# Transposes of x and of the selected rows in 64-row halves, a whole group of heads per visit

## The chip, the core and the metric

The kernel runs on one core of one Trainium2 chip. The metric is the device time of one execution in microseconds; the median of several runs is compared. TensorE is called PE in the views (PEld is its weight load), VectorE DVE, ScalarE ACT, GpSimd POOL, and SyncE, which issues most of the DMAs, SP. All data is float32.

## What is computed

Eight batches of 12 heads of normalised attention over 448 tokens with heads of 64 columns, and then, for each batch, a mixture of depths: a gate scores the 448 tokens, the 128 best go through a two-layer network of 1024 hidden columns, and the rest pass unchanged.

```
q_n, k_n = q / sqrt(mean(q*q) + 1e-6) * g_q,  k / sqrt(mean(k*k) + 1e-6) * g_k
attn = softmax(q_n @ k_n.T / sqrt(64))           # 8 x 12 x 448 x 448
x = (attn @ v)  as  (8, 448, 12 * 64 = 768)
scores = x @ w_gate                              # 8 x 448
top = indices of the 128 largest scores of a batch
out = x;  out[top] = x[top] + sigmoid(scores[top]) * (relu(x[top] @ w1) @ w2)
```

## The kernel before

The work is 24 groups of heads (8 batches of 3 groups, 4 heads each), and the main loop `for q in range(n_groups)` has a section for each group. In a section PE runs 7 steps; a step is `scores` (L445: keys times queries, 64x64 tiles, 448 columns) for a slice of 64 keys of each head, an exponential on ScalarE (L462), and `values` (L470) into two accumulators. Two steps of scores alternate with two of values, 16 matmul records each. When the last slice is done, `values_out` (L497) copies the two accumulators to SBUF as xT, heads by tokens.

`sum_keys` (L510) sums the exponentials over the keys on PE ("den") into the only bank of `ps_aux`; VectorE has added most of them beforehand (`add_probs`, L493). `invert_sums` (L540) transposes den on PE (L543) and takes the reciprocal on VectorE (L545). `to_tokens(n, c, pool)` (L568) then turns xT of one pair of heads c into x, tokens by columns: four transposes of 128 rows and 112 columns into one bank (L575), and one multiplication with the reciprocals from PSUM to SBUF on VectorE (L577), 112x512. It is called for c = 0 and c = 1 at different places. `after_tokens` schedules the stores of x and the gate products.

Sections 0 to 7 (`q < FIRST`) have two stops, place 0 after four steps and place 1 at the end. At place 0 stand `sum_keys(q - 1)` and pair 1 of group q - 2, at place 1 `invert_sums(q - 1)` and pair 0 of group q - 1, both in the bank of `ps_moe`. From section 8 on all this comes after the 7 steps, at P0, P1 and P2, and each of the three is followed by a piece of the mixture (`step(q, place)`) unless it is in SKIP. A mixture works on two batches at once: `xeT` (L772 to L787) transposes the two gathered blocks of 128 rows, four banks of three transposes of 128x128 each (L777) and four copies on ScalarE (L782); then 7 products for the first layer (L800, 128x128 tiles, `main` in `ps_moe`, `side` in `ps_sc`) and 7 for the second (L870). The fourth mixture and the end of the third run behind section 23.

Between the batches `gate` (L603), `score_rows` (four transposes, L633), `count` (L649), `annotate` and `select` rank the tokens; `select` scatters the chosen rows by POOL's DMA queue and `load_selected` (L699) reads them back on SP.

PSUM has 8 banks: `ps_sc` 4 (scores, side products, x, xeT, score rows), `ps_av` 2, `ps_aux` 1, `ps_moe` 1. A bank is reused when its last reader is done, and the banks of a pool go round in turn.

The order of the work is written out by hand: `at(slot, fn)` puts a piece into a table by due time, in units of sections, and `run(upto)` issues what is due (tables LOADS, PREPARED, STORES, GATES, RANKS). Each engine executes its instructions in the order of issue; DMA issues queue on SP in the same way, so that an issue that waits holds up those behind it. `Loads.load` (L131) keeps 6 buffers for `tok`, the tiles whose squares give the norms; a load into a buffer waits for the square (L345) of its last tile. The norms of the queries go by POOL (L380) and by DRAM (L391, L403) back as a broadcast, and `scale_q` (L409, L412) multiplies the queries with them on VectorE, which the first scores of the group need.

## Time and profile before

| | |
|---|---|
| median of 3 runs | 489.68 us (489.34 to 491.05) |
| the profiled execution | 488.96 us |
| its span | 487.2 us |
| mean granted clock of TensorE | 0.997 of full speed |
| DMA | 118.44 MB, mean 243 GB/s |

The span is the time from the first to the last instruction in the profile; the time of the execution has 1.8 us more. A row of the timeline is a run of equal instructions of one engine: start, length from the first one's start to the last one's end, engine, line, operation, output and inputs, and how many. Matmul records overlap: one lasts 0.27 us or more from issue to the end, while the next begins after its columns have gone through. Sections are found in the timeline by the den matmuls (L520), which stand once in each: place 0 of section 2 is at 42 us, section 8 ends at 131 us, section 23 at 409 us.

### The profile page before, as it was taken

Reading aid. Unit: us, or ns where it says so; the run is one execution under the profiler, and the core shown is the slowest. Engines: PE = TensorE matmul, PEld = TensorE weight load, DVE = VectorE, ACT = ScalarE, POOL = GpSimd, SP = SyncE. Lnnn points to the kernel's source line nnn. Section 1 sums busy time; section 2 is a strip of 40 time slices with the busy share of each in tenths; the row PEclk is TensorE's granted clock in tenths of the full one; section 3 lists DMA queues with packets and bytes.
Section 4 is the critical chain, followed back from the end, with each engine's and each line's share of the span. In section 5 each row is a group of like instructions: output and inputs, shape, how many; then the busy total and the mean of one; then the engine's idle time right before and its main releaser. Section 6 shows DMA issues by size and latency. Waiting matters only on the chain.

```text
span 487.2 us, 11747 instructions
## 1 busy us (share of the span) xinstructions
PE 477.4 (98%) x4708; PEld 294.4 (60%) x4708; DVE 370.2 (76%) x637; ACT 284.8 (58%) x523; POOL 193.2 (40%) x110
## 2 busy tenths in 40 slices
PE   8999999999999999999999999999999999999995
PEld 6554445445578856545557678555456746858962
DVE  5677789867989898998987887889777896753241
ACT  5887887887786566643854865656546574201200
POOL 0785444824652447313846234304183023032002
PEclk9999999999999999999999999999999999999998
DMA  8977879689789976987587876776648404766631
GB/s 300 364 228 279 299 267 277 238 298 320 259 292 369 342 259 193 350 268 266 198 281 283 296 232 230 254 259 219 206 142 279 149 2 122 253 206 249 194 132 71
DMA packets 45121, 118.44 MB, mean 243 GB/s; under 512 B 10275, under 2 KB 10788, under 8 KB 45058
## 3 DMA queue, kind: packets, MB, share of 16 engines
q1 hardware_dynamic: 41442, 110.66, 66.8%
q0 software_dynamic: 3328, 6.71, 4.2%
q8 instruction: 39, 0.64, 0.5%
q10 hardware_dynamic: 288, 0.23, 0.2%
q14 instruction: 24, 0.20, 0.1%
HBM read 93.81 MB, written 31.64 MB: 258 GB/s over the span
## 4 chain that ended last, share of the span: by engine, by line
PE 93%; DMA 4%; DVE 1%; ACT 0%; issue 0%; SPq 0%; POOL 0%; POOLq 0%; DVEq 0%
PE sc L453 26%; PE av L477 25%; PE moe_ps L800 9%; PE moe_ps L870 9%; PE side_ps L870 6%; PE side_ps L800 6%; PE x_ps L575 4%; PE den_ps L520 4%; DMA tok<-in_tok_dram 2%; DMA qT<-in_qT_dram 2%; PE xeT_ps L777 1%; PE row_ps L633 1%; PE den_ps L543 1%; DVE prod L603 0%; ACT sq L345 0%
## 5 line engine op out<-in xcount | busy, mean ns | idle before, releaser
L462 ACT ACTIVATE p<-sc,rinv 128x448 f32<-128x448 f32 x336 | 187.8, 643 | 83.3 <-PE sc L453 63.3
L380 POOL TENSOR_TENSOR rinv<-ss,neg_half 128x14 f32<-128x14 f32 x46 | 131.4, 2869 | 155.1 <-DVE ss L379 145.9
L453 PE MATMUL sc<-qT,kT 64*64 64x448 f32 x1344 | 155.0, 542 | 2.0 <-ACT sq L345 0.8
L477 PE MATMUL av<-p,v 64*64 64x448 f32 x1344 | 151.1, 537 | 0.0
L493 DVE TENSOR_TENSOR sum<-sum,p 128x896 f32<-128x896 f32 x104 | 113.4, 1090 | 5.1 <-ACT p L462 0.8
L477 PEld LDWEIGHTS av<-p,v 64*64 64x64 f32 x1344 | 64.0, 133 | 62.3 <-issue 52.8
L453 PEld LDWEIGHTS sc<-qT,kT 64*64 64x64 f32 x1344 | 58.4, 132 | 65.3 <-issue 42.2
L676 POOL DMA_INDIRECT selected<-x,rank x32 | 41.9, 1308 | 73.2 <-DVE x L668 65.7
L379 DVE TENSOR_REDUCE ss<-sq 128x14 f32<-128x910 f32 x46 | 49.0, 1093 | 8.5 <-ACT sq L345 8.5
L345 ACT ACTIVATE sq<-tok 128x896 f32<-128x896 f32 (+1 forms) x49 | 44.8, 939 | 6.9 <-DVE ss L379 3.4
L577 DVE TENSOR_TENSOR x<-x_ps,rden 112x512 f32<-112x512 f32 x48 | 32.7, 689 | 17.0 <-PE x_ps L575 15.3
L603 DVE SCALAR_TENSOR_TENSOR prod<-x,wg 112x448 f32<-112x448 f32 (+1 forms) x56 | 31.3, 558 | 1.5
L575 PE MATMUL x_ps<-ident,xT 128*112 128x128 f32 x192 | 28.7, 275 | 0.8 <-DVE rden L545 0.8
L412 DVE SCALAR_TENSOR_TENSOR qT<-qT,gg,bc 128x896 f32<-128x896 f32 x22 | 25.2, 1145 | 4.1 <-DMA bc<-rows 2.5
L493 DVE TENSOR_TENSOR sum<-p 128x896 f32<-128x896 f32 x24 | 26.0, 1084 | 2.2 <-ACT p L462 2.2
L500 ACT COPY xT<-av 128x448 f32<-128x448 f32 x48 | 23.2, 535 | 4.4 <-PE av L477 3.0
L575 PEld LDWEIGHTS x_ps<-ident,xT 128*112 128x112 f32 x192 | 21.5, 133 | 5.2 <-issue 2.5
L649 DVE SCALAR_TENSOR_TENSOR cmp<-score_rows,gate,earlier 112x448 f32<-112x448 f32 x32 | 21.8, 683 | 2.3 <-ACT score_rows L639 1.6
L800 PE MATMUL moe_ps<-xeT,ring 128*128 128x128 f32 x192 | 23.1, 277 | 0.0
L800 PE MATMUL side_ps<-xeT,w 128*128 128x128 f32 x192 | 22.8, 275 | 0.0
L743 DVE SCALAR_TENSOR_TENSOR xe<-moe_ps,xe 128x384 f32<-128x384 f32 x14 | 8.6, 616 | 18.2 <-PE moe_ps L870 18.2
L800 PEld LDWEIGHTS moe_ps<-xeT,ring 128*128 128x128 f32 x192 | 22.1, 192 | 0.5 <-issue 0.5
(105 smaller groups left out, 444.5 us busy)
## 6 DMA issues: line engine op xcount, KB each, us to landing
tok<-in_tok_dram SPq DMA_DIRECT2D x47, 448.0 KB
ring<-mixed SPq DMA_DIRECT2D x48, 384.0 KB
kT<-in_kT_dram SPq DMA_DIRECT2D x24, 448.0 KB
v<-in_vp_dram SPq DMA_DIRECT2D x24, 448.0 KB
out_dram<-x SPq DMA_DIRECT2D x16, 672.0 KB
qT<-in_qT_dram SPq DMA_DIRECT2D x23, 448.0 KB
bc<-rows SPq DMA_DIRECT2D x44, 224.0 KB
mixed<-ring SPq DMA_DIRECT2D x16, 384.0 KB
```

The lines of the kernel that those rows point to most:

```text
L345: nc.scalar.activation(out=sq[:, h, :, 0:D], in_=t[:, h], func=AF.Square, scale=scale)
L379: nc.vector.tensor_reduce(out=ss, in_=sq, axis=AX.X, op=OP.add)
L380: nc.gpsimd.tensor_tensor(out=rinv.rearrange(flat), in0=ss.rearrange(flat), in1=neg_half.to_broadcast([128, 2 * NI]), op=OP.pow,)
L453: nc.tensor.matmul(out=scs[hh][D * c : D * (c + 1), 0:S], lhsT=get("kT", n)[r, c, D * i : D * (i + 1)], rhs=get("qT", n)[r, c, :], start=True,
L462: nc.scalar.activation(out=p[:, hh], in_=scs[hh][:, 0:S], func=AF.Exp, scale=rinvs[n, 1][:, hh, i : i + 1],)
L477: nc.tensor.matmul(out=avs[n][c][D * hh : D * (hh + 1), 0:S], lhsT=get("v", n)[r, hh, i, :], rhs=probs[u][r, hh], start=(i == 0), stop=(i ...
L493: nc.vector.tensor_tensor(out=sums[n], in0=probs.pop(u - 1) if begins else sums[n], in1=probs.pop(u), op=OP.add)
L575: nc.tensor.transpose(out=ps[:CP, j, :], in_=t[:, j, :], identity=ident)
L577: nc.vector.tensor_tensor(out=xs[b][:, :, col : col + 128].rearrange("p j (h d) -> p j h d", d=D), in0=ps[:CP].rearrange("p j (h d) -> p j ...
L676: w = nc.gpsimd.indirect_dma_start(out=t[:, :], out_offset=bass.IndirectOffsetOnAxis(ap=rank[:, j : j + 1], axis=0), in_=x[:, j, :], in_of ...
L800: nc.tensor.matmul(out=ps[:, 128 * f : 128 * f + n], lhsT=w[:, d, 128 * f : 128 * (f + 1)], rhs=h[:, d, :n], start=first and f == d == 0, ...
L870: nc.tensor.matmul(out=ps[:n, 0:HD], lhsT=h[:, f, :n], rhs=w[:, f, :], start=first and f == 0, stop=(f == HF - 1), skip_group_check=True,)
```

## The change

- A new helper `transpose_halves` makes two transposes of 64 rows out of one of 128: rows 0 to 63 into one bank, 64 to 127 into another, each against a 64x64 identity. A transpose of x then moves 64 columns, one head, and not 128.
- `to_tokens(n, pools)` handles both pairs of a group at once: 8 double transposes into two banks, then two multiplications on VectorE of the same size as before, one for each bank.
- xeT is transposed in the same way: for each block two banks and six double transposes, two copies each.
- In sections 2 to 7 x is made once, at place 0, for group q - 2: `invert_sums(q - 2)`, `to_tokens(q - 2)`, then `sum_keys(q - 1)`. Place 1 keeps only the score rows, now for all batches.
- From section 10 on x is made at P1 in two banks of `ps_sc`; P2 and `ps_aux` have none any more. Sections 8 and 22 (NEXT) leave theirs to P0 of the section after, before its `sum_keys`.
- `tok` has 5 buffers instead of 6, xT 4 instead of 3. A load of tok is scheduled no earlier than the square of the tile five before. At the start the load of tok (2, 1) goes behind that of v 1.

```diff
-OTHER_BANK = (8, 14, 20, 21)
+NEXT = (8, 22)
-GATES = {8: (10.4, 10.4),
+GATES = {7: (9.75, 9.9),
+ 8: (10.4, 10.4),
-        bufs = {"tok": 6, "qT": 4, "kT": 3, "v": 3}[name]
+        bufs = {"tok": 5, "qT": 4, "kT": 3, "v": 3}[name]
+    def transpose_halves(halves, in_):
+        rows = in_.shape[0]
+        for h, out in enumerate(halves):
+            r = slice(D * h, min(D * (h + 1), rows))
+            nc.tensor.transpose(out=out, in_=in_[r], identity=ident[r, r])
-    load("tok", 2, 1)
     load("v", 1)
-            t = norm_pool.tile([128, NJ, CP], F32, name="xT", bufs=3)
+            t = norm_pool.tile([128, NJ, CP], F32, name="xT", bufs=4)
-    def to_tokens(n, c, pool):
+    def to_tokens(n, pools):
...
-        t = xTs.pop((n, c))
-        ps = bank(pool, [128, NJ, 128], "x_ps")
-        for j in range(NJ):
-            nc.tensor.transpose(out=ps[:CP, j, :], in_=t[:, j, :], identity=ident)
-        col = (n % NG * 2 + c) * 128
-        nc.vector.tensor_tensor(
-            out=xs[b][:, :, col : col + 128].rearrange("p j (h d) -> p j h d", d=D),
-            in0=ps[:CP].rearrange("p j (h d) -> p j h d", d=D),
-            in1=rdens[n][:, :, :, c, None].to_broadcast([CP, NJ, 2, D]),
-            op=OP.mult,
+        halves = [bank(pool, [128, NJ, 2, D], "x_ps") for pool in pools]
+        for c in range(2):
+            t = xTs.pop((n, c))
+            for j in range(NJ):
+                transpose_halves([ps[:CP, j, c, :] for ps in halves], t[:, j, :])
+        x = xs[b][:, :, n % NG * 256 : n % NG * 256 + 256].rearrange(
+            "p j (c h d) -> p j c h d", c=2, d=D
         )
+        for hh, ps in enumerate(halves):
+            nc.vector.tensor_tensor(
+                out=x[:, :, :, hh],
+                in0=ps[:CP],
+                in1=rdens[n][:, :, hh, :, None].to_broadcast([CP, NJ, 2, D]),
+                op=OP.mult,
+            )
+        after_tokens(n)
...
         for i, x in enumerate(xe):
-            for a in range(2):
-                ps = bank(ps_moe if a == i == 0 else ps_sc, name="xeT_ps")
-                for d in range(HC):
-                    dc = HC * a + d
-                    nc.tensor.transpose(
-                        out=ps[:, 128 * d : 128 * d + n],
-                        in_=x[:n, 128 * dc : 128 * (dc + 1)],
-                        identity=ident[:n, :n],
-                    )
+            halves = [
+                (slice(D * h, min(D * (h + 1), n)), bank(pool, [128, 512], "xeT_ps"))
+                for h, pool in zip(range((n + D - 1) // D), (ps_sc if i else ps_moe, ps_sc))
+            ]
+            for dc in range(NDC):
+                transpose_halves(
+                    [ps[:, D * dc : D * dc + t.stop - t.start] for t, ps in halves],
+                    x[:n, 128 * dc : 128 * (dc + 1)],
+                )
+            for t, ps in halves:
                 nc.scalar.copy(
-                    out=xeT[:, i, HC * a : HC * (a + 1), :n],
+                    out=xeT[:, i, :, t],
...
+                t = LOADS.get(("tok", n), n - 5 + P2 if n > 5 else (n - 3) * 0.6)
+                at(max(t, squared_at.get(2 * n + i - 5, 0) + 1e-4), load, "tok", n, i)
...
     keys = squares(0, 1)
+    load("tok", 2, 1)
...
                 if place == 0:
+                    if q > 1:
+                        invert_sums(q - 2)
+                        to_tokens(q - 2, (ps_sc, ps_moe))
                     if q > 0:
                         sum_keys(q - 1)
-                    if q > 1:
-                        to_tokens(q - 2, 1, ps_moe)
-                    if q > NG and g == 1 and b - 1 in GATE_PE:
-                        ranks_of(b - 1)
                 elif q == 0:
                     scale_q_early(1)
-                elif q > 0:
-                    invert_sums(q - 1)
-                    to_tokens(q - 1, 0, ps_moe)
-                    if q > NG and g == 1 and b - 1 not in GATE_PE:
-                        ranks_of(b - 1)
+                elif q > NG and g == 1:
+                    ranks_of(b - 1)
...
         slot[0] = q + P0
+        if q == FIRST:
+            invert_sums(q - 2)
+            to_tokens(q - 2, (ps_sc, ps_moe))
+        if q - 1 in NEXT:
+            if q - 1 == FIRST:
+                invert_sums(q - 2)
+            to_tokens(q - 2, (ps_sc, ps_sc))
         sum_keys(q - 1)
-        if q == FIRST:
-            to_tokens(q - 2, 1, ps_sc)
...
         slot[0] = q + P1
-        invert_sums(q - 1)
-        to_tokens(q - 1, 0, ps_sc)
+        if q != FIRST:
+            invert_sums(q - 1)
+        if q not in NEXT:
+            to_tokens(q - 1, (ps_sc, ps_sc))
         run(q + P1)
         step(q, 1)
         slot[0] = q + P2
-        to_tokens(q - 1, 1, ps_sc if q in OTHER_BANK else ps_aux)
...
     invert_sums(n)
-    to_tokens(n, 0, ps_sc)
-    to_tokens(n, 1, ps_aux)
+    to_tokens(n, (ps_sc, ps_sc))
```

## Rows read from the trace of the kernel before

**Rows 1.** The page, part 1: busy us, share of the span, instructions.

```profile
PE 477.4 (98%) x4708; PEld 294.4 (60%) x4708; DVE 370.2 (76%) x637; ACT 284.8 (58%) x523; POOL 193.2 (40%) x110
```

**Rows 2.** The page, part 4: the chain that ended last, by line.

```profile
PE sc L453 26%; PE av L477 25%; PE moe_ps L800 9%; PE moe_ps L870 9%; PE side_ps L870 6%; PE side_ps L800 6%; PE x_ps L575 4%; PE den_ps L520 4%; DMA tok<-in_tok_dram 2%; DMA qT<-in_qT_dram 2%; PE xeT_ps L777 1%; PE row_ps L633 1%; PE den_ps L543 1%; DVE prod L603 0%; ACT sq L345 0%
```

**Rows 3.** Timeline of PE, section 1: start us, us, engine, line, operation, tiles, count.

```profile
34.50 0.93 PE L477 MATMUL av<-p,v 64*64 64x448 f32 x8
35.36 0.32 PE L543 MATMUL den_ps<-ident,den 128*112 128x128 f32 x1
35.52 0.60 PE L575 MATMUL x_ps<-ident,xT 128*112 128x128 f32 x4
36.05 1.73 PE L453 MATMUL sc<-qT,kT 64*64 64x448 f32 x16
37.60 1.68 PE L477 MATMUL av<-p,v 64*64 64x448 f32 x16
```

**Rows 4.** Timeline of PE, end of section 11 and the scores of 12.

```profile
183.33 0.59 PE L520 MATMUL den_ps<-sum,pick_pair 128*32 128x112 f32 x16
183.85 2.94 PE L800 MATMUL moe_ps<-xeT,ring 128*128 128x128 f32 x24
...
186.74 0.60 PE L575 MATMUL x_ps<-ident,xT 128*112 128x128 f32 x4
187.75 0.65 PE L575 MATMUL x_ps<-ident,xT 128*112 128x128 f32 x4 [0.40 <-DVE rden L545]
188.23 2.84 PE L800 MATMUL moe_ps<-xeT,ring 128*128 128x128 f32 x24
191.00 1.73 PE L453 MATMUL sc<-qT,kT 64*64 64x448 f32 x16
```

**Rows 5.** Groups of instructions by form: busy us, mean ns, idle before.

```profile
L477 PEld LDWEIGHTS av<-p,v 64*64 64x64 f32 x1344 | 64.0, 133 | 62.3 <-issue 52.8 <-ACT xT L500 0.6
...
L575 PE MATMUL x_ps<-ident,xT 128*112 128x128 f32 x192 | 28.7, 275 | 0.8 <-DVE rden L545 0.8
...
L800 PEld LDWEIGHTS side_ps<-xeT,w 128*128 128x128 f32 x192 | 22.1, 192 | 0.0
...
L575 PEld LDWEIGHTS x_ps<-ident,xT 128*112 128x112 f32 x192 | 21.5, 133 | 5.2 <-issue 2.5 <-DVE rden L545 2.2 <-DVE parts L666 0.2
...
L777 PEld LDWEIGHTS xeT_ps<-ident,xe 128*128 128x128 f32 x42 | 4.6, 141 | 0.8 <-issue 0.7
...
L423 PE MATMUL sc<-ident,rinv 64*64 64x64 f32 x112 | 3.6, 221 | 0.0
```

**Rows 6.** Timeline of PE at the start: the products of line 423.

```profile
7.04 1.67 PE L423 MATMUL sc<-ident,rinv 64*64 64x64 f32 x56
```

**Rows 7.** Timeline of DVE: single rows of sections 5, 9 and 11.

```profile
85.17 0.69 DVE L577 TENSOR_TENSOR x<-x_ps,rden 112x512 f32<-112x512 f32 x1 [0.59 <-PE x_ps L575]
...
149.78 1.14 DVE L412 SCALAR_TENSOR_TENSOR qT<-qT,gg,bc 128x896 f32<-128x896 f32 x1
...
187.79 0.69 DVE L577 TENSOR_TENSOR x<-x_ps,rden 112x512 f32<-112x512 f32 x1
...
189.41 1.14 DVE L412 SCALAR_TENSOR_TENSOR qT<-qT,gg,bc 128x896 f32<-128x896 f32 x1
```

**Rows 8.** Timeline of PE: den of section 5, scores of 10, score rows at the end.

```profile
82.43 0.59 PE L520 MATMUL den_ps<-sum,pick_pair 128*32 128x112 f32 x16
...
151.72 1.90 PE L453 MATMUL sc<-qT,kT 64*64 64x448 f32 x16
...
422.16 0.59 PE L633 MATMUL row_ps<-ident,gate 112*112 112x112 f32 x4 [0.43 <-DVE gate L616]
```

**Rows 9.** Timeline of ACT: two squares of tok, the copies of the last xeT.

```profile
147.82 0.95 ACT L345 ACTIVATE sq<-tok 128x896 f32<-128x896 f32 x1 [1.68 <-issue]
...
189.53 0.95 ACT L345 ACTIVATE sq<-tok 128x896 f32<-128x896 f32 x1 [3.37 <-DVE ss L379]
...
443.87 1.63 ACT L782 COPY xeT<-xeT_ps 128x384 f32<-128x384 f32 x4 [17.79 <-PE xeT_ps L777]
```

More of the change, by code (lines that the diff above doesn't have):

```diff
@@ L571, in to_tokens @@
             xs[b] = x_pool.tile([CP, NJ, DX], F32, name="x")
-        t = xTs.pop((n, c))
-        ps = bank(pool, [128, NJ, 128], "x_ps")
-        for j in range(NJ):
-            nc.tensor.transpose(out=ps[:CP, j, :], in_=t[:, j, :], identity=ident)
-        col = (n % NG * 2 + c) * 128
-        nc.vector.tensor_tensor(
-            out=xs[b][:, :, col : col + 128].rearrange("p j (h d) -> p j h d", d=D),
-            in0=ps[:CP].rearrange("p j (h d) -> p j h d", d=D),
-            in1=rdens[n][:, :, :, c, None].to_broadcast([CP, NJ, 2, D]),
-            op=OP.mult,
-        )
-        if c == 1:
-            after_tokens(n)
+        halves = [bank(pool, [128, NJ, 2, D], "x_ps") for pool in pools]
[5 more added lines that the diff above has]
+            "p j (c h d) -> p j c h d", c=2, d=D
+        )
+        for hh, ps in enumerate(halves):
[6 more added lines that the diff above has]
+        after_tokens(n)
     gates, parts, rowss, highers, ranks, slots_dram = {}, {}, {}, {}, {}, {}
@@ L772, in mixture @@
         for i, x in enumerate(xe):
-            for a in range(2):
-                ps = bank(ps_moe if a == i == 0 else ps_sc, name="xeT_ps")
-                for d in range(HC):
-                    dc = HC * a + d
-                    nc.tensor.transpose(
-                        out=ps[:, 128 * d : 128 * d + n],
-                        in_=x[:n, 128 * dc : 128 * (dc + 1)],
-                        identity=ident[:n, :n],
-                    )
+            halves = [
[8 more added lines that the diff above has]
+            for t, ps in halves:
                 nc.scalar.copy(
-                    out=xeT[:, i, HC * a : HC * (a + 1), :n],
-                    in_=ps[:, : HC * 128].rearrange("p (i t) -> p i t", t=128)[:, :, :n],
+                    out=xeT[:, i, :, t],
+                    in_=ps[:, : NDC * D].rearrange("p (i t) -> p i t", t=D)[
+                        :, :, : t.stop - t.start
+                    ],
                 )
@@ L926, in fast @@
     MID, P0, P1, P2 = 0.4, 0.6, 0.75, 0.9
+    squared_at = {}
     def prepare(n):
@@ L946, in prepare @@
         for i in range(2):
+            squared_at[2 * n + i] = times[f"sq{i}"]
             at(times[f"sq{i}"], lambda i=i: sq.setdefault(i, squares(n, i)))
@@ L955, in fast @@
             for i in range(2):
-                at(LOADS.get(("tok", n), n - 5 + P2 if n > 5 else (n - 3) * 0.6), load, "tok", n, i)
+                t = LOADS.get(("tok", n), n - 5 + P2 if n > 5 else (n - 3) * 0.6)
+                at(max(t, squared_at.get(2 * n + i - 5, 0) + 1e-4), load, "tok", n, i)
         if n > 1:
```

## The prediction

> **What bounds the kernel now.** I read the busy times first [rows 1]: TensorE is busy 98% of the span, VectorE 76%, ScalarE 58%. The chain of work that ended last [rows 2] says that TensorE is the bound and not only full: nearly all of the chain is PE lines, and the transposes of x (L575) are 4% of it, some 20 us, those of xeT (L777) 1%. So a microsecond less of PE work is a microsecond less of time, until something that PE now covers comes last; VectorE is the nearest. The PE timeline then shows what a transpose costs and what an interruption costs [rows 3, 4].
>
> **A transpose now.** Four of x take 0.60 us and one alone 0.27, so one follows another in 0.11 us [rows 3, 5]; there are 192, 8 to a group of heads. xeT has 48, 12 to each of four mixtures.
>
> **The halves.** No transpose of 64 rows is in the trace. The nearest rows are the 64x64 products of line 423: two row halves in turn, each into its own bank, 64 columns moving, as in the new helper. 56 of them take 1.67 us and one lasts 0.22, so (1.67 - 0.22)/55 = 0.026 us each, 0.053 a pair [rows 5, 6]; I take 0.055. Eight pairs then take 0.44 us in place of 8 x 0.11 = 0.87: 0.43 saved for each of 24 groups, 10.3 us. xeT: 12 pairs 0.66 in place of 1.31, 0.65 x 4 = 2.6 us. Bounds: 0.053, and 0.11 if the halves run one after another. What differs from line 423 is the stationary side, 112 or 128 columns instead of 64. Its loads last 133 ns (112) and 141 (128) for transposes, 133 (64) and 192 (128) for plain products [rows 5]: 8 ns for 16 columns, 0.5 a column, against 59 for 64, 0.9 a column. 112 columns at 0.5 are 56 ns, about a pair. So I stay near the lower bound.
>
> **The price of another tile shape.** Whenever PE goes from one tile shape to another, the trace has a hole [rows 3]. In section 1, 8 values matmuls from 34.50 should end at 35.25 (16 take 1.50); the den transpose is at 35.36, its record 0.05 longer than 0.27. Four x transposes from 35.52 should end at 35.96; the scores come at 36.05 and their record is 1.73, not 1.68 as the next burst's. Each such change costs about 0.14. Into a plain 128x128 product it is 0.20: moe begins 0.1 late after den (16 take 0.4) and its record is 2.94, not 2.84 [rows 4]. Into den, whose stationary side is 32 columns, I take 0.11. Between x and moe, both of 128 rows, there is no hole now: 188.23 is 0.48 behind an x burst that started 0.05 late [rows 4]. In the new kernel every burst of 64 rows stands between work of other shapes. The trace has no change between 64 and 128 rows at these columns; its price lies between 0 and 0.20, and I take 0.14 in and 0.20 out to a product, since every change of shape that the trace shows costs that. The Trainium skill (TensorEngine Tiling, Key Properties) says that changing the tiling mode, and not just the tile, drains TensorE. The trace agrees for the pairs of shapes it holds; by that rule the price taken stands.
>
> **Section by section** (a section works on one group of heads; its first part ends at place 0, its second at place 1). Section 1: the interruption at place 1 goes, 0.14 + 0.11 + 0.44 + 0.14 = 0.83; the rows give 0.85. Sections 2 to 7: old, x at both places, 0.11 + 0.14 + 0.44 + 0.14 and 0.83, together 1.66 beside the den matmuls; new, one visit: 0.14 + 0.11 (den transpose) + 0.14 + 0.44 + 0.11 + 0.14 = 1.08. Gain 0.58 each; in 4 and 7 the score rows now need an interruption of their own, 0.28, which leaves 0.30. Sum 0.85 + 4 x 0.58 + 2 x 0.30 = 3.8. Section 8: 12 transposes become 8 pairs and group 7 waits for section 9: +0.7. Section 9 takes groups 7 and 8, xeT and six more changes of shape: 2.7 us of such work becomes 2.9, -0.2. Sections 10 to 21: 0.43 - 0.14 - 0.20 = 0.09 each, 0.9 for ten; in 15 and 21, which have xeT, 0.09 + 0.65 - 0.14 = 0.6 each. Section 22 hands its x (0.87) to 23: +0.9; 23 then has two bursts of halves, -0.3. Behind the last section x is shorter by 0.4. All that: 3.8 + 0.7 - 0.2 + 0.9 + 1.2 + 0.9 - 0.3 + 0.4 = 7.4.
>
> **What comes late instead**, each bounded by nothing and by twice the number given.
> - Section 9: scaling group 10's queries on VectorE (L412) ends at 150.92; the scores that need it start at 151.72 [rows 7, 8]. Two more evacuations and a reciprocal for group 7 and two of its gate products (some 3 us) now stand before it there. -1.0.
> - Section 11: a wait of PE goes. The second x burst starts at 187.75, 0.6 late, for the one bank of ps_aux, which rden's reciprocal holds [rows 4]; the new code takes two of ps_sc. But both evacuations (0.69 each) then stand before scaling group 12, now 189.41 to 190.55 with scores at 191.00 [rows 4, 7]: it ends near 191.1. The 0.6 and the 0.09 are lost: -0.2 against the sum.
> - Halves want two banks of ps_sc; where xeT came just before (sections 9, 15, 21), one is held by its second copy, two of four that take 1.63 [rows 9]: -0.35 each, 1.1.
> - Section 5: the den matmuls now wait for a reciprocal issued just before them, since ps_aux has one bank. VectorE was free only 0.59 us before 85.17, while den started at 82.43 [rows 7, 8]; the work moved out of section 4 gives back 1.6. -0.5. At place 0 of the other early sections its queue is shorter.
> - Last section: the score rows at 422.16 already wait for the gate on VectorE [rows 8], whose evacuations end no earlier: the 0.4 is lost.
> - Last xeT: the products behind it needed one copy, now two: both halves ready 0.7 after the start, two copies some 0.85 [rows 9], 1.6 against 1.31 now: -0.3. (Its 0.65 is not in the sum.)
>
> Together 1.0 + 0.2 + 1.1 + 0.5 + 0.4 + 0.3 = 3.5. So 7.4 - 3.5 = 3.9 us.
>
> **Free edits.** VectorE's evacuations stay two of 512 columns to a group, ScalarE's xeT copies four of 384. The fourth xT buffer costs memory only. Five tok buffers instead of six: a load waits on SP until ScalarE has squared the tile five earlier, and SP's later rows, broadcasts and loads queue behind it. The worst, counting loads and squares in the code's order, is tok (14, 1) in section 9: its predecessor is squared at 147.82, its own square is at 189.53 [rows 9], so 40 us of work hide it. At the start tok (2, 1) goes one place back, behind v 1. Price 0, at most 1 us if the first sections then wait for it. The ranks of batch 1 move to place 1 of section 7; the gather that they release on POOL's queue is for the xeT of section 9. Price 0, and if that cover were gone, the 3 us by which they move.
>
> **The sum** against the profiled execution (488.96; span 487.2 and 1.8 around it) is 488.96 - 3.9 = 485.1. That execution lies 0.7 below the median of 489.68, so the forecast is 489.68 - 3.9 = **485.8**, and on its own 483.3 to 488.3: most of the waits absent, or twice as large but for a third.
>
> **Rivals.**
> - *The change of shape to 64 rows is free* where the columns stay 128. Then 22 changes in (0.14), 14 out to products (0.20) and those about xeT (0.8) go: 6.7 us, less some 0.5 that VectorE's scaling then holds up: 479.6. For it: x to moe is free at equal rows. Against: all other changes cost.
> - *VectorE takes most of it.* Scaling ends 0.8 and 0.45 us before the scores in sections 9 and 11; PE that comes earlier waits for it, and in section 5 the reciprocal waits for a whole backlog: another 2.5 us, 488.3. Against: VectorE idles a quarter of the span.
> - *The weight loads bound the pair; slower.* At 0.9 ns a column, as plain loads have it, 112 columns are 0.10 us and 128 are 0.12, so a pair takes what one whole transpose took: the 12.9 us of shorter bursts are gone, the changes of shape stay, and the waits (some 2.5 us) mostly do not arise: 485.8 + 12.9 - 2.5 = 496. It decides from a pair of about 0.08 us on. For it: nothing shows loads of 112 columns side by side. Against: the transposes' loads grow half as fast [rows 5]. The same time comes out if the change does not do what it says and the halves run one after another; line 423 speaks against that [rows 6]. The Trainium skill (TensorE: Matmul & The Clock Gate, LDWEIGHTS) gives columns over 1.2 GHz for a load, whatever its rows; by that estimate 112 columns are 93 ns and this rival holds. The trace has 8 ns for the last 16 columns of a transpose's load where that rule has 13.
>
> **How the numbers follow.** Forecast 0.57, free changes 0.12, VectorE 0.19, weight loads or halves in turn 0.12. Half a per cent, about what a measurement of this kernel can tell from no change, is 2.4 us: faster means under 487.2, slower over 492.1. Faster: four fifths of the forecast, free changes, a little of VectorE's case, 0.60; same 0.27; slower 0.13. The range reaches from 480.0, just above the free changes, to 491.5, past VectorE's case; the slower rival and most of the free changes lie outside, two in ten.
>
> **What will show it.** Eight pairs of x in about 0.44 + 0.2 us as a record: right; near 0.9: the slower rival. The hole between the den transpose and the first half, and between the last half and moe: 0.14 and 0.20, or none. A wait of scores for L412 in sections 9 and 11, of den for L545 in 5. PE starved by tok in the first sections would make the free edits wrong.

## The result, and the profile after

The changed kernel takes 496.17 us (median of 4 runs, 495.82 to 496.98) against 489.51 (488.82 to 491.05) on the same chip: a ratio of 1.0137, 95% interval 1.0121 to 1.0153. It is slower by 1.4%, where 485.8 was forecast, and lies outside the range. The profiled execution took 496.08, its span is 494.4 at a granted clock of 0.998. The page's busy times, and its chain by line:

```profile
PE 477.1 (97%) x4948; PEld 294.3 (60%) x4948; DVE 370.5 (75%) x637; ACT 283.6 (57%) x523; POOL 188.3 (38%) x110
...
PE av L484 11%; PE sc L460 11%; PE moe_ps L883 8%; PE moe_ps L813 7%; PE side_ps L813 4%; PE side_ps L883 4%; PE den_ps L527 1%; PE x_ps L232 1%; DVE x L588 1%; DVE prod L613 1%; ACT xeT L793 1%; PE row_ps L643 0%; DVE xeT L763 0%; PE xeT_ps L232 0%; DVE xe L753 0%
```

Against [rows 1], PE is busy as long as before in a span that is 7.2 us longer: it is not the work that grew. Against [rows 2], this chain holds lines of VectorE and ScalarE between those of PE (L588, L613, L793, L753), and it stops half way through the span, so it can't be read to the start. The waits of PE in the trace of after (us in total, times, longest) say for whom:

```profile
PE sc L460 <- DVE xe L753: 1.9, 3, 1.0
PE row_ps L643 <- DVE gate L626: 1.2, 1, 1.2
...
PE den_ps L527 <- issue: 1.0, 3, 0.4
...
PE sc L460 <- PE moe_ps L813: 0.7, 1, 0.7
```

The first and the third have no like in the kernel before. They don't add up to 7 us, because each idle time is followed by bursts that run longer than before. So I measured sections whole, from the first scores of one to the first scores of the next. "23 and behind" ends with the start of PE's last instruction. The table gives before's length, and then the changes against it in us: as the prediction has them, and as the profiled executions of after and of five of the experiments have them.

| section | before | predicted | after | E1 | E5 | E6 | E8 | last version |
|---|---|---|---|---|---|---|---|---|
| start and 0 | 23.46 | 0 | +0.28 | +0.31 | +0.85 | +0.48 | +2.22 | +0.19 |
| 1 to 3 | 38.63 | -2.01 | -1.73 | -1.74 | -1.73 | -1.79 | -1.75 | -1.80 |
| 4 | 14.17 | -0.30 | +0.06 | +0.06 | +0.06 | +0.39 | +0.06 | -0.03 |
| 5 | 14.17 | -0.08 | **+2.19** | +2.28 | -0.41 | -0.41 | -0.40 | -0.25 |
| 6, 7 | 27.71 | -0.88 | -0.58 | -0.60 | -0.59 | -0.59 | -0.60 | -0.54 |
| 8 | 13.56 | -0.70 | -0.08 | +3.47 | +1.20 | +1.48 | -0.09 | -0.16 |
| 9 | 20.03 | +1.55 | +1.36 | +0.64 | -0.08 | -0.38 | +1.35 | +0.64 |
| 10 | 20.92 | -0.09 | **+0.81** | +1.77 | -0.08 | +0.01 | +0.81 | -0.08 |
| 11 | 18.36 | +0.11 | +0.24 | +0.25 | +0.24 | 0 | +0.25 | +0.24 |
| 12, 16, 17, 18, 20 | 94.40 | -0.45 | -0.48 | -0.46 | -0.48 | -0.10 | -0.47 | -0.46 |
| 13 | 18.65 | -0.09 | **+1.83** | -0.08 | +1.83 | 0 | +1.83 | -0.08 |
| 14 | 18.57 | -0.09 | **+1.86** | -0.34 | +0.18 | -0.49 | +0.19 | -0.34 |
| 15, 21 | 38.02 | -0.50 | -0.26 | -0.25 | -0.25 | 0 | -0.26 | -0.26 |
| 19 | 20.47 | -0.09 | **+1.54** | +0.47 | +1.53 | 0 | +1.54 | +0.46 |
| 22 | 13.14 | -0.90 | -1.00 | -1.00 | -1.00 | 0 | -1.00 | -1.03 |
| 23 and behind | 86.90 | +0.60 | +1.28 | +1.42 | +1.15 | 0 | +1.15 | +0.74 |
| sum | 481.15 | -3.9 | +7.3 | +6.2 | +2.4 | -1.4 | +4.8 | -2.7 |

Five sections are off by nearly a microsecond or more: 5, 10, 13, 14, 19. The others came out within 0.4 us, but for 8 and 23 (0.6 and 0.7).

**The halves themselves.** By form (busy us, mean ns of one, idle before), then PE's timeline of sections 11 and 12, to lay beside [rows 4] and [rows 5]:

```profile
L232 PE MATMUL x_ps<-ident,xT 64*112 64x64 f32 x384 | 16.6, 223 | 0.4
L232 PEld LDWEIGHTS x_ps<-ident,xT 64*112 64x112 f32 x384 | 12.9, 130 | 6.2 <-PE moe_ps L883 1.6 <-issue 1.4 <-ACT xeT L793 0.8
```

```profile
189.13 0.66 PE L232 MATMUL x_ps<-ident,xT 64*112 64x64 f32 x16
189.86 2.94 PE L813 MATMUL moe_ps<-xeT,ring 128*128 128x128 f32 x24
193.54 1.74 PE L460 MATMUL sc<-qT,kT 64*64 64x448 f32 x16 [0.73 <-PE moe_ps L813]
...
207.81 0.27 PE L550 MATMUL den_ps<-ident,den 128*112 128x128 f32 x1
208.02 0.66 PE L232 MATMUL x_ps<-ident,xT 64*112 64x64 f32 x16
208.60 2.85 PE L883 MATMUL side_ps<-w,hT 128*128 128x384 f32 x8
```

Sixteen halves are one record of 0.66, the last one of them 0.22: 0.44 for 15 steps, 0.029 each, a pair in 0.059. In section 12 nothing waits: the first half comes 0.21 behind the den transpose, where a transpose comes 0.11 behind another; the product comes 0.58 behind the first half, 0.11 more than 16 x 0.029, and its record is 0.11 longer than the 2.74 of the next. So a change in costs 0.10 and one out 0.22. All of x is 16.6 us of matmul time where [rows 5] has 28.7. Section 11 has its x at one visit of 0.73, with the stop of [rows 4] gone, and pays ahead of the scores at 193.54.

**Section 5 and the scores of section 13.** In section 5 PE stops four times among the den matmuls, for no releaser that the trace shows, while GpSimd starts the first gathers:

```profile
82.01 0.59 PE L527 MATMUL den_ps<-sum,pick_pair 128*32 128x112 f32 x16
82.39 1.14 PE L527 MATMUL den_ps<-p,pick_pair 128*32 128x112 f32 x35
83.88 0.40 PE L527 MATMUL den_ps<-p,pick_pair 128*32 128x112 f32 x6 [0.35 <-issue]
84.60 0.40 PE L527 MATMUL den_ps<-p,pick_pair 128*32 128x112 f32 x4 [0.33 <-issue]
85.34 0.29 PE L527 MATMUL den_ps<-p,pick_pair 128*32 128x112 f32 x2 [0.34 <-issue]
...
86.09 0.63 PE L536 MATMUL den_ps<-xT,hT 128*32 128x112 f32 x14 [0.33 <-issue]
```

```profile
82.58 1.16 POOL L686 DMA_INDIRECT selected<-x,rank  x1 [0.19 <-issue]
```

In section 13 the wait has a name. After, VectorE and PE (the two x evacuations, six gate products, then xe, which empties the side product's bank for the second unit of scores):

```profile
210.83 1.29 DVE L588 TENSOR_TENSOR x<-x_ps,rden 112x512 f32<-112x512 f32 x2
...
212.16 0.62 DVE L613 SCALAR_TENSOR_TENSOR prod<-x,wg 112x448 f32<-112x448 f32 x1
...
213.96 1.71 PE L460 MATMUL sc<-qT,kT 64*64 64x448 f32 x10
...
215.09 0.49 DVE L613 SCALAR_TENSOR_TENSOR prod<-x,wg 112x320 f32<-112x320 f32 x1
...
215.97 0.61 DVE L753 SCALAR_TENSOR_TENSOR xe<-side_ps,xe 128x384 f32<-128x384 f32 x1
...
216.63 0.60 PE L460 MATMUL sc<-qT,kT 64*64 64x448 f32 x3 [0.96 <-DVE xe L753]
```

The same place before, where two of six products and xe stood ahead of the second evacuation:

```profile
210.24 0.61 DVE L743 SCALAR_TENSOR_TENSOR xe<-side_ps,xe 128x384 f32<-128x384 f32 x1
...
211.37 0.69 DVE L577 TENSOR_TENSOR x<-x_ps,rden 112x512 f32<-112x512 f32 x1
211.52 1.73 PE L453 MATMUL sc<-qT,kT 64*64 64x448 f32 x16
```

xe was done before the first scores began; now it starts 2 us behind them.

### The profile page after: what moved, and what is told of

It is laid out like the page before. It is cut to its first block, busy times and chain, and to the rows that moved or that the text cites. A ratio compares the mean times of both kernels' runs of the same rounds, so it can differ in the third digit from the quotient of the medians.

```text
span 494.4 us, 12222 instructions
## 1 busy us (share of the span) xinstructions
PE 477.1 (97%) x4948; PEld 294.3 (60%) x4948; DVE 370.5 (75%) x637; ACT 283.6 (57%) x523; POOL 188.3 (38%) x110
## 4 chain that ended last, share of the span: by engine, by line
PE 48%; DVE 3%; ACT 1%; issue 0%; POOL 0%; DVEq 0%; POOLq 0%
PE av L484 11%; PE sc L460 11%; PE moe_ps L883 8%; PE moe_ps L813 7%; PE side_ps L813 4%; PE side_ps L883 4%; PE den_ps L527 1%; PE x_ps L232 1%; DVE x L588 1%; DVE prod L613 1%; ACT xeT L793 1%; PE row_ps L643 0%; DVE xeT L763 0%; PE xeT_ps L232 0%; DVE xe L753 0%
## 5 line engine op out<-in xcount | busy, mean ns | idle before, releaser
L460 PE MATMUL sc<-qT,kT 64*64 64x448 f32 x1344 | 162.6, 543 | 5.7 <-DVE xe L753 1.9
L484 PE MATMUL av<-p,v 64*64 64x448 f32 x1344 | 155.8, 537 | 0.0
L460 PEld LDWEIGHTS sc<-qT,kT 64*64 64x64 f32 x1344 | 64.4, 132 | 71.7 <-issue 40.5
L484 PEld LDWEIGHTS av<-p,v 64*64 64x64 f32 x1344 | 68.5, 133 | 58.5 <-issue 44.7
L686 POOL DMA_INDIRECT selected<-x,rank x32 | 38.0, 1189 | 80.4 <-DVE x L678 72.9
L386 DVE TENSOR_REDUCE ss<-sq 128x14 f32<-128x910 f32 x46 | 49.2, 1093 | 11.2 <-ACT sq L352 7.5
L588 DVE TENSOR_TENSOR x<-x_ps,rden 112x512 f32<-112x512 f32 x48 | 30.9, 687 | 7.5 <-PE x_ps L232 3.0
L613 DVE SCALAR_TENSOR_TENSOR prod<-x,wg 112x448 f32<-112x448 f32 (+1 forms) x56 | 31.2, 556 | 1.3
L419 DVE SCALAR_TENSOR_TENSOR qT<-qT,gg,bc 128x896 f32<-128x896 f32 x22 | 25.2, 1145 | 0.6 <-issue 0.6
L753 DVE SCALAR_TENSOR_TENSOR xe<-moe_ps,xe 128x384 f32<-128x384 f32 x14 | 8.6, 617 | 19.3 <-PE moe_ps L883 19.3
L883 PE MATMUL side_ps<-w,hT 128*128 128x384 f32 x64 | 22.3, 491 | 0.0
L883 PE MATMUL moe_ps<-ring,xeT 128*128 128x384 f32 x64 | 22.2, 490 | 0.0
```

Of the source, the lines that this page charges most:

```text
L386: nc.vector.tensor_reduce(out=ss, in_=sq, axis=AX.X, op=OP.add)
L460: nc.tensor.matmul(out=scs[hh][D * c : D * (c + 1), 0:S], lhsT=get("kT", n)[r, c, D * i : D * (i + 1)], rhs=get("qT", n)[r, c, :], start=True,
L484: nc.tensor.matmul(out=avs[n][c][D * hh : D * (hh + 1), 0:S], lhsT=get("v", n)[r, hh, i, :], rhs=probs[u][r, hh], start=(i == 0), stop=(i ...
L588: nc.vector.tensor_tensor(out=x[:, :, :, hh], in0=ps[:CP], in1=rdens[n][:, :, hh, :, None].to_broadcast([CP, NJ, 2, D]), op=OP.mult,)
L613: nc.vector.scalar_tensor_tensor(out=prod[:, 0 : cols.stop - cols.start], in0=xs[b][:, j, cols], scalar=1.0, in1=wg[:, cols], op0=OP.mult, ...
L686: w = nc.gpsimd.indirect_dma_start(out=t[:, :], out_offset=bass.IndirectOffsetOnAxis(ap=rank[:, j : j + 1], axis=0), in_=x[:, j, :], in_of ...
```

## The experiments

My theory after the result: two causes. VectorE's list has a new order, since `after_tokens` now runs once for the whole group at P1, and gate products and counts whose due time has already come go out at once, ahead of the share that empties a bank; and section 5 has stops of another kind, beside the gathers. Rivals: the halves cost more than they save, or the halves bring the stops. The kernel before was run again beside the experiments: 488.96 us with E1 to E4, 488.51 with E5 to E7 and the first mended version, 488.77 with E8, E9 and the last version. Each ratio is against that.

**E1, other due times alone.**

```diff
-GATES = {7: (9.75, 9.9),
+GATES = {7: (10.4, 10.4),
...
- 11: (12.75, 12.75),
+ 11: (12.9, 12.9),
...
- 17: (18.75, 18.9),
+ 17: (18.9, 18.9),
...
-RANKS = {2: (10.9, 10.9, 10.9, 11.3), 5: (19.6, 20.3, 20.3, 20.4), 6: (22.9, 23.4, 23.4, 23.9)}
+RANKS = {2: (10.9, 10.9, 10.9, 11.3), 3: (13.6, 13.9, 13.9, 14.3), 5: (19.6, 20.3, 20.3, 20.4), 6: (22.9, 23.4, 23.4, 23.9)}
```

> Only due times are moved: the gate products of groups 7, 11 and 17 and the last counts of batch 3 go behind the piece of the mixture that is issued at place 1, so that VectorE empties the bank of the side product before them. Theory (the order of VectorE's list): the second unit of scores no longer waits in sections 10, 13, 14 and 19, which give back 0.8, 1.9, 1.9 and 1.6, and section 9 about 0.5: some 6 us, 489.5 to 491. Rival (the two banks): halves of both pairs hold two banks of ps_sc until both evacuations are done, whatever VectorE does later; then the scores go on waiting and the time stays within 1 us of the changed kernel's 496.2. Section 5 is untouched: its four stops of some 0.6 us within the den matmuls should show again if they belong to the kernel and not to one execution.

491.43 us (491.13 to 495.04), ratio 1.0045 (1.0028 to 1.0062): 4.7 us less than after (4.5 by the ratios). The wait for xe is gone; sections 13 and 14 are back (14 without its stop, too), 19 by 1.07. What is left in 19 is, as the rows read, the evacuations of x, ahead of xe still; VectorE begins to empty the side bank 0.65 us behind the first scores. Moving group 7's products from section 9 to 10 gave 0.72 and took 0.96: eight products now stand ahead of the gate that the score rows wait for. Section 5 keeps its stops.

```profile
329.49 1.92 PE L460 MATMUL sc<-qT,kT 64*64 64x448 f32 x13
...
330.14 0.61 DVE L753 SCALAR_TENSOR_TENSOR xe<-side_ps,xe 128x384 f32<-128x384 f32 x1
```

```profile
PE row_ps L643 <- DVE gate L626: 3.0, 2, 1.8
```

Its profiled execution took 495.04 where the other four took 491.1 to 491.6: it alone has one stop of ScalarE in section 8, also beside gathers (123.0 to 127.8), which makes that section's +3.47:

```profile
128.97 1.68 ACT L469 ACTIVATE p<-sc,rinv 128x448 f32<-128x448 f32 x3 [4.15 <-PE av L484]
```

**E2, whole transposes in the new places and banks.** The pieces of the change apart: `transpose_halves` back to one transpose of 128 rows, for x and xeT, all else as changed.

```diff
...
-                transpose_halves([ps[:CP, j, c, :] for ps in halves], t[:, j, :])
...
+                nc.tensor.transpose(out=ps[:CP, j, :], in_=t[:, j, :], identity=ident)
...
```

> The changed kernel with whole transposes of 128 rows again, at the new places and with the new banks (one bank for each pair), for x and for xeT: only the halves are undone. Theory (halves save what they should, the loss is in the placement): the waits of the scores in sections 10, 13, 14 and 19 stay, each late section is about 0.1 longer, each early one about 0.2, the sections with xeT 0.5, the last mixture 0.3 shorter: 3 us more than the changed kernel, less the 2 us of section 5 if its stops come from the number of PE instructions, so 497 to 499.5. Rival (halves themselves cost, by the changes of shape or by a bank more): 494 or less.

497.88 us (497.64 to 498.39), ratio 1.0184 (1.0167 to 1.0201): 1.7 us more than after (2.3 by the ratios). So the halves save, 0.05 to 0.28 in each of sections 2 to 7 but 5, and 0.08 to 0.13 in seven late ones, and the new places are what loses. The stops of section 5 are there without halves, though it is 0.50 shorter than in after:

```profile
83.15 1.28 PE L527 MATMUL den_ps<-p,pick_pair 128*32 128x112 f32 x33
84.78 0.62 PE L527 MATMUL den_ps<-p,pick_pair 128*32 128x112 f32 x15 [0.34 <-issue]
85.62 0.46 PE L536 MATMUL den_ps<-xT,hT 128*32 128x112 f32 x8 [0.22 <-issue]
```

**E3, the gathers of batch 0 later.**

```diff
-RANKS = {2: (10.9, 10.9, 10.9, 11.3), 5: (19.6, 20.3, 20.3, 20.4), 6: (22.9, 23.4, 23.4, 23.9)}
+RANKS = {0: (4.9, 4.9, 5.9, 6.5), 2: (10.9, 10.9, 10.9, 11.3), 5: (19.6, 20.3, 20.3, 20.4), 6: (22.9, 23.4, 23.4, 23.9)}
```

> The changed kernel with the ranks and the four gathers of batch 0 one section later, so that POOL issues no gather while the den matmuls of section 5 run. Two theories of the four stops of PE there (some 2.1 us): if the gathers cause them, they go and the time falls by about 2 us to 494; if PE's instructions come too slowly for 16 halves and 80 den pairs in a row, they stay, and the time stays within 0.5 us of 496.2.

494.75 us (494.11 to 495.29), ratio 1.0116 (1.01 to 1.0133). Section 5 takes 13.76, without stops; but section 6, where the gathers now run, is 0.99 longer, with ScalarE idle 0.89 ahead of the copies of xT. Here the stop goes where the gathers go.

**E4, whole transposes of x in section 5 alone** (the two forms behind an `if now[0] == 5`).

> The changed kernel with whole transposes of x in section 5 alone. If the number of PE instructions ahead of the den matmuls causes the four stops, 8 pairs fewer should let most of the 2.1 us go, less 0.2 for the longer burst: 494.3. If the gathers, or the load on the DMA queues at that time, cause them, they stay: 496.2 to 496.6.

494.33 us (493.61 to 495.4), ratio 1.0103 (1.0086 to 1.012). Section 5 takes 13.96, no stops, though the gathers run beside its den matmuls (the first one starts 0.45 behind them, 0.57 in after, and takes 2.54 instead of 1.16). That looks as if halves were to blame, which E2 denies; and here the start and section 0 happened to be 1.9 us longer too, with first scores at 10.91, so E4 alone decides nothing. Section 14 keeps its stop (20.37).

**E5, section 8 makes its own x.**

```diff
-NEXT = (8, 22)
+NEXT = (22,)
...
-GATES = {7: (9.75, 9.9),
- 8: (10.4, 10.4),
+GATES = {8: (10.4, 10.4),
...
-        if q != FIRST:
-            invert_sums(q - 1)
+        invert_sums(q - 1)
```

> The changed kernel, but group 7's x is transposed in section 8, in halves, as every other group's is in the section behind its own, and not in section 9 beside group 8's; its gate products take their times of the kernel before. Theory (VectorE's list in section 9 is what costs: two more evacuations and a reciprocal, and two gate products, stand ahead of the scaling of group 10's queries and of the emptying of the side bank): sections 8 to 10, 56.6 in the changed kernel and 54.5 in the kernel before, come to 54 to 54.7, so the whole falls by 2 to 2.5 us to 494. Rival (the bank that xeT's second copy holds, and the changes of shape, cost most of it): sections 8 to 10 stay above 56 and the whole within 0.7 of 496.2.

490.55 us (490.48 to 491.43), ratio 1.0041 (1.0026 to 1.0057). Sections 9 and 10 are back at -0.08 each, so moving group 7 into 9 had cost 2.3. Section 8 gives 1.28 of it back: with one bank in `ps_aux` the den matmuls wait for the reciprocal just ahead of them, and the den transpose for ScalarE's copy:

```profile
128.50 0.59 PE L526 MATMUL den_ps<-sum,pick_pair 128*32 128x112 f32 x16 [0.59 <-DVE rden L551]
...
130.23 0.32 PE L549 MATMUL den_ps<-ident,den 128*112 128x128 f32 x1 [0.37 <-ACT den L543]
```

The larger part of the gain was not planned: section 5 has no stops (13.76), and section 14 is 1.68 shorter. Up to section 8 this kernel issues the same instructions as after; its first scores come 0.57 later, which no edit explains.

**E6, only sections 1 to 7 as changed,** from 8 on whole transposes, pair by pair in the old places.

> One part alone: sections 1 to 7 as changed (both pairs in one visit, in halves), everything from section 8 on as in the kernel before, in whole transposes at two places. By the early sections of the two profiles this gives 0.80, 0.50, 0.43, -0.06, -2.19, 0.30 and 0.28, 0.06 in all, and about 0.4 more for the later visit of group 6: 489 to 490, no change. If the late sections had only passed on what the early ones lost (buffers and loads shifted in time), the loss would show here too: 492 or more.

486.71 us (486.71 to 487.33), ratio 0.9964 (0.9951 to 0.9977). The early part of the change alone is a gain: 2.4 us in sections 1 to 7, of which section 8, where the two ways meet, takes 1.48. Section 5 has halves and gathers here, and no stops. Section 14, whose code is that of the kernel before, is 0.49 shorter than there: the kernel before has a stop of ScalarE in it that E6 lacks, so this part of the gain is not the change's.

**E7, no gathers in section 5.** Batch 0's four indirect gathers become plain transfers of its first 128 rows by SP, so the selection is left out.

> The changed kernel without the four gathers of batch 0 (its selected rows are left out: the first 128 rows of tokens are written in their place by plain transfers of SP's queue), with everything else, the ranks too, where it was. Theory (the gathers on POOL beside the den matmuls are what stops PE in section 5): no stops, section 5 about 13.9 instead of 16.4, section 6 not longer than 12.7: some 494. Rival (the moved ranks of the earlier run changed something else, and PE's instructions come too slowly there): the stops stay, 496.

492.02 us (491.91 to 492.24), ratio 1.0071 (1.0056 to 1.0087). Section 5 takes 13.76, no stops. But section 14 takes 18.75, though its gathers are as in after, so the missing gathers need not be what made the difference in section 5. Section 9 is 0.47 longer than in after; the others are as they were, within 0.22. First scores here are at 9.57, next to E2's 9.62 and after's 9.78, which have the stops.

**E8 and E9, after with a later start.** Six, and twelve, idle memsets on VectorE ahead of the first scaling of queries, so that all behind them moves and the order of the instructions stays.

```diff
+    for _ in range(6):
+        nc.vector.memset(pick_pair, 0.0)
     scale_q_early(0)
```

> The changed kernel with six small memsets of VectorE ahead of the first scaling of queries, so that all that follows starts some half a microsecond later; TensorE, ScalarE, POOL and SP have the same instructions in the same order. The kernel with group 7's x in section 8 had the same instructions up to there, the same gathers beside the same den matmuls, started 0.57 us later, and had no stops in section 5. If the stops (2.6 us there, and ScalarE's 1.0 us in section 14, which costs 1.7) come from how the streams happen to lie against each other, they can vanish here and the time falls to about 492 to 494; if they belong to the halves and the gathers, it is 496.7, the delay more.

> The same with twelve memsets, a start of about one microsecond later. By the theory of chance alignment the stops of section 5 and of section 14 are there or not, each by itself, and the time is 0.5 to 1 us above that of the changed kernel less 0, 2.6, 1.7 or 4.3; if the stops belong to the kernel, 497.2.

E8: 493.39 us (492.85 to 493.62), ratio 1.009 (1.0071 to 1.0108). E9: 494.24 (493.98 to 494.58), 1.0109 (1.0091 to 1.0127). More work, and less time than after: the start and section 0 are 1.94 us longer in E8, section 5 is 2.59 shorter and 14 is 1.67 shorter; all others are within 0.05 but the last one, 0.13. In E9 the first scores are at 11.65, section 5 is the same as in E8, section 14 at 19.00. Not all of the 1.94 is the shift. The first scores come 1.15 later, and then run slower: PE, idle for 2.22 us ahead of them, has a granted clock of 0.50 (1.2 GHz) between 12 and 14 us, where after has 1.00. E9 has such a stretch (0.56), and E4, without any memset. First after, then E8:

```profile
9.78 3.80 PE L460 MATMUL sc<-qT,kT 64*64 64x448 f32 x24 [1.06 <-DVE qT L439]
```

```profile
10.93 4.62 PE L460 MATMUL sc<-qT,kT 64*64 64x448 f32 x24 [2.22 <-DVE qT L439]
```

Section 5 in E8, PE and GpSimd, where the den matmuls run through; the first gather starts 0.56 behind the den matmuls, in after 0.57:

```profile
83.93 0.59 PE L527 MATMUL den_ps<-sum,pick_pair 128*32 128x112 f32 x16
84.31 1.36 PE L527 MATMUL den_ps<-p,pick_pair 128*32 128x112 f32 x48
85.46 0.59 PE L536 MATMUL den_ps<-xT,hT 128*32 128x112 f32 x16
```

```profile
84.49 1.16 POOL L686 DMA_INDIRECT selected<-x,rank  x1 [0.19 <-issue]
```

And ScalarE ahead of the copies of xT in section 14, first of after, then of E8, then of E4:

```profile
239.64 0.97 ACT L507 COPY xT<-av 128x448 f32<-128x448 f32 x2 [1.00 <-PE sc L460]
```

```profile
238.30 0.97 ACT L507 COPY xT<-av 128x448 f32<-128x448 f32 x2 [0.36 <-PE sc L460]
```

```profile
238.93 0.97 ACT L507 COPY xT<-av 128x448 f32<-128x448 f32 x2 [0.95 <-PE sc L460]
```

E4 and E8 have the same work in section 14 at nearly the same time: its scores begin at 233.79 and 233.75, its first gather at 235.48 and 235.45. Yet E4 has the stop and E8 has not, so neither the start nor how the engines lie against each other in these rows decides it.

So of section 14's excess 1.67 us goes with the stop (after against E8) and some 0.53 is the wait for xe (E8 against E1, where the gathers there moved too).

**A first mended version:** E1's times for 11, 17 and the counts of 3, E5, whole transposes in section 5 and for the last xeT, and the score rows behind section 23 one product later.

> What the runs so far suggest, together: the changed kernel with the gate products of groups 11 and 17 and the last counts of batch 3 behind the piece of the mixture; group 7's x in section 8; whole transposes in section 5 and for the xeT of the last mixture; the score rows of the last batch one product later, where their gate is ready. By sections against the changed kernel: 4.9 for 13, 14 and 19, 2.2 for 8 to 10, 2.4 for 5, 0.3 for the last xeT, 1.2 for the score rows: 11 us, 485.2, some 4 us faster than the kernel before. If the waits only move on to another bank, 488 or more.

487.40 us (486.64 to 488.3, 11 runs), ratio 0.9976 (0.9967 to 0.9985). The rows' wait went, but subtractions then stood behind the counts and the next product waited 1.06 us: section 23 and behind took 88.67, the longest of all.

**The last version:** the same without that step, and with group 7's x made in section 8 between its den matmuls and its den transpose, its reciprocal already in section 7.

```diff
+                    if q == FIRST - 1:
+                        invert_sums(q - 1)
...
-        if q == FIRST:
-            invert_sums(q - 2)
-            to_tokens(q - 2, (ps_sc, ps_moe))
...
         sum_keys(q - 1)
+        if q == FIRST:
+            to_tokens(q - 2, (ps_sc, ps_moe))
```

> A version that should beat both: the changed kernel with the gate products of groups 11 and 17 and the last counts of batch 3 behind the piece of the mixture; group 7's x in section 8, where group 6's denominators are turned in section 7 already and its x lies between the den matmuls and the transpose of group 7's denominators, so that neither waits for a reciprocal or a copy; whole transposes in section 5 and for the xeT of the last mixture. Against the kernel before, by sections: 2.6 less in 1 to 7, nothing in 8 to 10, 0.3 less from 11 to 21, nothing behind: 485.5. If the wait in section 8 only changes its place, 487.

486.20 us (486.05 to 487.37), ratio 0.9954 (0.9938 to 0.9969): it beats both kernels. By the ratios it can't be told from E6 (0.9964), which has the old whole transposes in the old places from section 8 on. And some 0.3 us of the gain is section 14, where the kernel before has the stop that this execution lacks. Section 8 takes 13.40; section 9 keeps 0.64, since its scores now wait for the evacuation of x:

```profile
130.69 1.20 PE L459 MATMUL sc<-qT,kT 64*64 64x448 f32 x5 [0.58 <-DVE x L601]
```

## Why the prediction failed

**What held.** A pair costs 0.059 (0.055 taken). The changes of shape cost 0.10 in and 0.22 out (0.14 and 0.20). Five late sections with nothing in their way gained 0.48 where 5 x 0.09 was worked out, section 22 gained 1.00 (0.9), sections 1 to 3 gained 1.73 (2.01). So the rival in which this change of shape is free falls, and so does the one in which the weight loads bound the pair. It gave 496, the time that came, and is still wrong: two loads of 112 columns come every 0.059 us, where the rule cited from the Trainium skill (TensorE: Matmul & The Clock Gate, LDWEIGHTS) would have each take 93 ns, by the prediction's estimate. The measurement decides against it here. The Trainium skill's TensorEngine Tiling, Key Properties, by which a change of mode drains TensorE, agrees with the holes of 0.10 and 0.22 in section 12.

**Late terms that held.** Section 9 was to lose 1.0 for the scaling of group 10's queries and 0.35 for a bank after xeT; both are there: the record of the x halves is 1.04 instead of 0.66, and scores wait for a scaling that ends at 153.10 (PE and VectorE of after, sections 9 and 10):

```profile
145.97 1.04 PE L232 MATMUL x_ps<-ident,xT 64*112 64x64 f32 x16
...
151.96 1.14 DVE L419 SCALAR_TENSOR_TENSOR qT<-qT,gg,bc 128x896 f32<-128x896 f32 x1
...
153.21 2.40 PE L460 MATMUL sc<-qT,kT 64*64 64x448 f32 x13 [0.64 <-issue]
...
155.10 0.68 DVE L830 TENSOR_TENSOR hT<-hT,side_ps 128x512 f32<-128x512 f32 x1
```

In section 11 the same holds: scores at 193.54 against a scaling (L419) of VectorE, 192.30 to 193.44. The profile puts that wait down to moe_ps, which had ended at 192.80. In the last section the score rows wait 1.19 for the gate, so the saving in x is lost there as forecast, and the last xeT's products wait 0.57 for a copy, and start 0.31 later behind the product ahead of the transposes than before (0.3 forecast):

```profile
429.10 0.56 PE L643 MATMUL row_ps<-ident,gate 112*112 112x112 f32 x4 [1.19 <-DVE gate L626]
...
451.88 1.38 PE L813 MATMUL moe_ps<-xeT,w 128*128 128x128 f32 x10 [0.57 <-ACT xeT L793]
```

**The first step that failed** is the sentence that sections 10 to 21 gain 0.09 each. It follows x on PE and looks on VectorE only for the scaling of the next queries. What else `after_tokens` brings to VectorE was left out: called once at P1 instead of at P2, it releases gate products and counts whose due times were written for the old place, ahead of the side product's emptying (L753, in section 10 L830 at 155.10 above). The bank that this frees is the second unit of scores'. By E1 that is 1.91 in section 13, some 0.53 in 14 (E8 against E1) and 1.07 in 19; 0.47 more in 19 is, as E1's rows read and no run tested, the evacuations themselves, and in 10 it is 0.89 by E5. Together 4.9 us. The rival "VectorE takes most of it" named the engine, but at 2.5 us and by way of the scaling and of section 5's reciprocal; the latter, put at 0.5, turned up in section 8 of E5 instead.

**The second step** is one that was not there: the stops in section 5 (2.6 us, after against E8) and section 14 (1.67), 4.3 us. Their cause is open. In section 5 the change moved the first gather from 3.29 us behind the start of the den matmuls to 0.57, but E5 and E8 have that place too and no stops, so whether the change brought them or bad luck is not shown. The kernel without them is E8 less its later start: 493.39 - 1.94 = 491.45, against 488.77 for the kernel before beside it. So without this cause the change would still have been no gain, and E1, with the order mended and the stops of section 5 left, is at 491.43 (488.96 before). Only E6 and the two mended versions, without the stops and without group 7's x in section 9, gain.

**Sizes.** Section 8 was 0.6 short: 8 scores and 8 values there take 1.23 and 1.07 where the kernel before has 0.93 and 0.93 (0.44), and den waits 0.15 for a reciprocal.

```profile
127.41 1.23 PE L460 MATMUL sc<-qT,kT 64*64 64x448 f32 x8
128.46 1.07 PE L484 MATMUL av<-p,v 64*64 64x448 f32 x8
...
130.53 0.59 PE L527 MATMUL den_ps<-sum,pick_pair 128*32 128x112 f32 x16 [0.15 <-DVE rden L552]
```

Section 4 lost 0.36 in such slower bursts. Why they run slower I didn't follow. 23 and behind lost 0.7 more than forecast, sections 1 to 3, 6 and 7, and the start 0.3 each, 15 and 21 0.24, 11 0.13, together 2.9. With 4.9 and 4.3 that is 12.1; the stretches that came out better (5 without its stops by 0.3, 14 by 0.25, 9 by 0.2, 22 by 0.1) take 0.9 off, which leaves the 11.2 between the table's +7.3 and -3.9.

**The free edits** were free as far as the runs tell: behind the start nothing waits for tok, and sections 1 to 3 came out within 0.3 us. At the start ScalarE waits 1.11 us for a tile of tok, where it waited 0.65 before, and the first scores come 0.31 later. In other executions with the same first instructions they come at 9.57 (E7) to 10.91 (E4), so this is within what one execution differs from another.

## What to carry to other kernels

When a step is moved, what it schedules moves too: go through each engine's list at the new place, up to the next instruction that frees a bank or a buffer, and not only along the step's own data. A hand-written table of due times is right for one order, so a new order is judged only after the table has been put right: the same change was 1.4% slower with the old times and, with the few steps that lost left out and no stops met, 0.5% faster. Before a loss is put down to a part of the change, run the changed kernel with a shifted start: a loss that goes away with the shift is not the fixed cost of that part, though the shift does not say what it is.

## What was not expected of the hardware

PE stops four times for 0.33 to 0.35 us in section 5 of after (2.6 us with the slower pace about the stops), with nothing in the trace that releases it. ScalarE stops in section 14 of after (idle for 1.00, where E8 has 0.36) and once in E1 (4.15). There the rows name PE, but the copies of xT start 0.74 us after the last values matmul had ended, where E8 has 0.09. Section 14 of E2 and E3 has yet another: the copies are on time, and PE is idle 0.55 a little later.

Every such stop that I saw lies beside gathers on GpSimd or begins some 1 us behind the last of them (after's sections 5 and 14, E2's 5 and 14, E3's 6 and 14, E4's 14, E1's 5 and 8; and section 14 of the kernel before, ScalarE idle 1.03 ahead of 234.69, which E6 doesn't have). That the gathers cause them is not shown: with the gathers of section 5 taken out its stops are gone (E7), but section 14's are too, with its gathers in place, and gathers at the same distance to the same instructions also pass without a stop (E5, E6, E8, E9).

The start does not explain it either. Executions with stops in section 5 had their first scores between 9.62 and 9.81 us, while those with gathers there from 9.98 on had none; but neither had the two mended versions at 9.76 and 9.69, which have whole transposes there, and E4 and E8 differ in section 14 at starts of 10.91 and 10.93. Instruction loading, as far as its DMA packets show it, is no answer: in the trace of after none starts between 75 and 86 us, and in E4's none between 230 and 245.

Whether the stops of a kernel come back in each execution is inferred from times alone: the four runs of after lie within 1.2 us, while E1's stop in section 8 can stand in one run of five only, since the others took 3.4 us less or better. What decides stays open: it was not isolated.
